# A bilinear GLU behind a dilated attention on one core: the up product copied by ScalarE in part of the steps, and due products placed earlier on VectorE

## The chip, the cores and the metric

The kernel runs on one core of a Trainium2 chip. The metric is device time in microseconds (us) of one execution. Three runs of the kernel before took 1050.43, 1051.01 and 1051.36 us, so the median is 1051.01 us. The engines are named as in the profile: PE (TensorE, with PEld for its weight loads), DVE (VectorE), ACT (ScalarE), POOL (GpSimd) and SP (the engine that issues the DMAs).

## The reference

Four layers work on x, which has 2048 tokens of 576 numbers. Layers 1 and 3 are attention (`_A_ref`), layers 2 and 4 a gated linear unit (`_B_ref`); the layers of a kind share their weights.

```
def _B_ref(x, w_gate, w_up, w_down):
    g = jnp.einsum("bsd,df->bsf", x, w_gate)
    u = jnp.einsum("bsd,df->bsf", x, w_up)
    h = g * u
    return jnp.einsum("bsf,fd->bsd", h, w_down)
...
x = x + _A_ref(_layernorm(x, axis=-1), A_wqkv, A_wo)
x = x + _B_ref(_layernorm(x, axis=-1), B_w_gate, B_w_up, B_w_down)
x = x + _A_ref(_layernorm(x, axis=-1), A_wqkv, A_wo)
x = x + _B_ref(_layernorm(x, axis=-1), B_w_gate, B_w_up, B_w_down)
```

In the attention each token looks at eight positions (its own and every second one before it) in 32 heads of 18 numbers. In the unit, F is 4608: the gate and the up product have 4608 columns each, and the down product leads back to 576.

## The kernel before, in words

**Steps.** The work is cut into 17 steps j, each one attention and one GLU on a block of tokens. Steps 0 and 1 take 128 tokens, all others 256. Steps 0 to 4 are layers 1 and 2 of the first 1024 tokens, 5 to 8 layers 3 and 4 of the same tokens, 9 to 12 and 13 to 16 the same for the last 1024 tokens.

**GLU of a step of 256 tokens** (`glu`, line 906). The 36 slices of 128 columns make 18 units of two slices; six units form a phase. A unit holds one slot: a PSUM bank for the gate (`pg`) and one for the up product (`pu`); there are four slots (the fourth pair of banks is called `acct` and `pa`). Two units at a time go through four "quarters" on PE (line 947): first quarter of unit m, of unit m+1, second quarter of m, of m+1. In each quarter two matmuls of 64 rows run beside each other, one on the gate, one on the up product. Between the first and second quarter of a unit ACT copies one number to `tok` (line 493); PE's second quarter waits for this token. After the second quarter `evac` (line 960) is called: ACT copies the gate from PSUM to `g_sb` (two buffers, line 964), and DVE multiplies the up product in PSUM with it into the bf16 tile `h` (six buffers, line 965), which also frees the slot. The down products of a phase (`down2`, line 1010, matmuls of lines 1021 and 1022) read `h` six units at a time, in two halves that hold two slots; the second half runs after the first quarter of the next phase. DVE then adds the sums to the residual stream `xf` (line 1001), which frees those two slots. Steps 0 and 1 have units of four slices, three to a phase, with matmuls of 128 rows (lines 929, 940 and 981) and no tokens.

**Attention of a step** (`attention`, line 515). PE projects (line 549), ACT brings q, k and v from PSUM to SBUF (lines 633 to 660), DVE forms the products of q and k (lines 727 to 713), takes the softmax with one exponential on ACT (lines 745 to 760), and the weights go through DRAM and back (`a_dram`, lines 791 to 796) to be spread over the partitions; in steps 0 to 2 (`on_pe`) PE spreads them instead (line 781) and ACT copies them to SBUF. Then DVE multiplies v with the weights and sums up, 16 long instructions (lines 811 and 833). PE applies the output weights (line 855), DVE adds the residual (line 846, which frees two slots), and the layer norm for the GLU follows (DVE 417, ACT 443, transposed by DMA or, in the first steps, by PE).

**What sets the order.** The program is written out by a planner (`Plan`, line 33). Every operation has an engine, a cost and dependencies; `run` takes the operation that can start first by its reckoning, and each engine runs its operations in the order in which they were taken. So the order on an engine is fixed, and an instruction that waits holds up all behind it. Each operation has a rank: an attention operation that of its step (line 1128), a GLU operation 60 (line 1130), and operations marked `due` have -1 (tokens, gate copies, products of line 965, residual additions of line 846). When the planner is about to place an operation of rank above 0, it looks for more urgent ones on the same engine (lines 119 to 125):

```
end = best[0][0] + o.cost
ahead = [(c[1].rank, c[0], c[1]) for c in urgent[o.eng] if c[1].rank < o.rank and c[1].rank < LOOK[o.eng]
         and c[0][0] < end + GUARD[o.eng] * (c[1].rank == 0) - SLACK[o.eng] * (c[1].rank < 0)
         and c[0][0] < best[0][0] + IDLE[min(max(c[1].rank, 0), 1)]]
```

LOOK is 1 on DVE, ACT and PE; SLACK is 500 (ns) on DVE and 300 on ACT; IDLE is 2000 for due operations. So a due operation is put ahead of a longer one if it can start at least 500 ns (DVE) before that one would end. Only operations whose predecessors have all been placed are candidates.

Of the kernel before, what the change touches and what calls it, by code (L numbers as in the profile page):

```python
# [10 lines left out]
ACT = mybir.ActivationFunctionType  # L11
ALU = mybir.AluOpType
# [3 lines left out]

class Op:
    __slots__ = ("eng", "cost", "fn", "deps", "order", "succ", "n", "prio", "idx", "hold", "free",
                 "lat", "margin", "ready", "end", "nbytes", "use", "pair", "need", "rank", "late", "half")


POOLQ = False
# [3 lines left out]
SLACK = {"DVE": 500, "ACT": 300, "PE": 0, "POOL": 0, "SP": 0}  # L26
IDLE = (2000, 300)
GUARD = {"DVE": 300, "ACT": 300, "PE": 600, "POOL": 0, "SP": 0}
# [4 lines left out]
class Plan:  # L33
# [11 lines left out]
        self.rd = {}  # L45

    def op(self, eng, cost, fn, r=(), w=(), prio=1, after=None, hold=None, free=None, margin=0, nbytes=0, use=None,
           pair=None, need=None, due=False, late=0, half=False):
        o = Op()
        o.rank, o.late, o.half = -1 if due else self.rank, late, half  # L50
        o.eng, o.cost, o.fn, o.prio, o.hold, o.free = eng, cost, fn, prio, hold, free
        o.margin, o.idx, o.succ, o.order, o.nbytes = margin, len(self.ops), [], set(), nbytes
        o.lat, o.use, o.pair, o.need = self.LAT[eng], use, pair, need
        d = set()
        for k in r:
            d.update(self.wr.get(k, ()))
        for k in w:
            d.update(self.wr.get(k, ()))
            d.update(self.rd.get(k, ()))
        for k in r:  # L60
            self.rd.setdefault(k, []).append(o)
        for k in w:
            self.wr[k] = [o]
            self.rd[k] = []
        d.discard(o)
        o.deps = d
        if after is not None and after not in d:
            o.order.add(after)
        for p in d | o.order:
            p.succ.append(o)  # L70
        o.n = len(d | o.order)
        self.ops.append(o)
        return o
# [10 lines left out]
    def run(self, slots):  # L84
        clock = {e: 0.0 for e in self.LAT}
        dma = {"SP": 0.0, "POOL": 0.0}
        free = {k: [(0.0, i) for i in range(v)] for k, v in slots.items()}
        cand = [o for o in self.ops if o.n == 0]
        done = 0
        half = False  # L90
        while cand:
            best = None
            urgent = {}
            for o in cand:
                t = 0.0
                for p in o.deps:
                    e = p.ready if p.eng != o.eng else p.end
                    if e > t:
                        t = e
                t += o.margin  # L100
                if o.hold is not None:
                    f = free[o.hold]
                    if not f:
                        continue
                    t = max(t, min(f)[0] + o.margin)
                if o.pair is not None:
                    if len(free["unit"]) < len(o.pair):
                        continue
                    t = max(t, min(free["unit"])[0] + o.margin)
                if o.need is not None:  # L110
                    t = max(t, o.need["at"])
                t = max(t, clock[o.eng])
                key = (t, o.prio, o.idx)
                if best is None or key < best[0]:
                    best = (key, o)
                urgent.setdefault(o.eng, []).append((key, o))
            assert best is not None, "the plan is stuck"
            o = best[1]
            if o.rank > 0:
                end = best[0][0] + o.cost  # L120
                ahead = [(c[1].rank, c[0], c[1]) for c in urgent[o.eng] if c[1].rank < o.rank and c[1].rank < LOOK[o.eng]
                         and c[0][0] < end + GUARD[o.eng] * (c[1].rank == 0) - SLACK[o.eng] * (c[1].rank < 0)
                         and c[0][0] < best[0][0] + IDLE[min(max(c[1].rank, 0), 1)]]
                if ahead:
                    best = min(ahead, key=lambda c: c[:2])[1:]
            (t, _, _), o = best
            cand.remove(o)
            if o.hold is not None:
                got = min(free[o.hold])
                free[o.hold].remove(got)  # L130
                o.use["slot"] = got[1]
            if o.pair is not None:
                for u in o.pair:
                    got = min(free["unit"])
                    free["unit"].remove(got)
                    u["at"], u["slot"] = got
            if o.eng == "PE" and self.fill and o.cost:
                if o.rank == 60:
                    self.fill = None
                else:  # L140
                    each = 430 if clock["PE"] < 5500 else 215
                    n = int((t - max(clock["PE"], 900) - 150) * 0.75 / each)
                    if n > 0:
                        self.fill(n)
            o.end = t + o.cost
            if o.eng == "PE" and o.cost:
                o.end += TURN[o.half] * (o.half != half)
                half = o.half
            clock[o.eng] = o.end
            o.ready = o.end + o.lat  # L150
            if o.nbytes:
                dma[o.eng] = max(dma[o.eng], o.end) + o.nbytes / (320.0 if o.eng == "SP" else 200.0)
                o.ready = dma[o.eng] + 2000 + o.late
            if o.free is not None:
                u = o.use
                u["last"] = max(u.get("last", 0.0), o.ready)
                u["left"] = u.get("left", 1) - 1
                if u["left"] == 0:
                    free[o.free].append((u["last"], u["slot"]))
            o.fn()  # L160
            done += 1
            for s in o.succ:
                s.n -= 1
                if s.n == 0:
                    cand.append(s)
        assert done == len(self.ops)
# [3 lines left out]
def kernel(  # L170
# [12 lines left out]
    nc = tc.nc  # L183
    _, S, D = A_x.shape
# [31 lines left out]
    def sb(name, shape, dt=BF16):  # L216
# [29 lines left out]
    oT = sb("oT", [P, KT, CH])  # L246
    n_al = nlayers // 2
    halo = [sb(f"halo{i}", [P, 2, KT, HALO]) for i in range(n_al)]
    hb = [sb(f"h{i}", [P, 2 * CH]) for i in range(NH)]
    g_sb = [sb(f"g_sb{i}", [P, 2 * CH]) for i in range(2)]  # L250
# [4 lines left out]
    pu = [psum.tile([P, 2 * CH], FP32, name=f"pu{i}") for i in range(NB)]  # L255
# [8 lines left out]
    late = {"prod": [scr[:, 2560 * i:2560 * (i + 1)].rearrange("p (a k s) -> p a k s", a=2, k=KT) for i in range(2)],  # L264
            "s1": [scr[:, o:o + 512].rearrange("p (a s) -> p a s", a=2) for o in (5120, 9216, 9728, 6656)],
            "a_c": scr[:, 6656:7168],
            "Lt": scr[:, 5632:6656].bitcast(FP32),
            "ab": scr[:, 7168:9216].rearrange("p (j s) -> p j s", j=4)}

    pl = Plan()  # L270
    op = pl.op
# [243 lines left out]
    def attention(j, la, t0, nst):  # L515
# [3 lines left out]
        on_pe = j < 3  # L519
        prio, mg = (1, 0) if fast else (3, 500 if j < 5 else 1200)  # L520
        n, sq = nst * P, nst * P // 4
# [144 lines left out]
        else:  # L666
# [12 lines left out]
           r=zk("k0", "k2", "k4", "v0", "v2", "v4"), w=hk, prio=prio)  # L679
# [18 lines left out]
        for p_ in range(W // 2):  # L698
# [26 lines left out]
            if nst == 2:  # L725
                for e in range(2):
                    op("DVE", 70 + 2.6 * n, lambda p_=p_, e=e: nc.vector.tensor_tensor(  # L727
                        late["prod"][p_ % 2][:, e, :, 0:n], qT[:, :, 0:n], kT[:, :, HALO - DIL * (2 * p_ + 1 - e):HALO - DIL * (2 * p_ + 1 - e) + n], op=ALU.mult),
                       r=qk, w=[pk], prio=prio)
            else:  # L730
                op("DVE", 70 + 5.2 * n, l1, r=qk, w=[pk], prio=prio)
            if fast:
                kw = b1.take() if p_ == 0 else dict(w=[b1.key])
                op("PE", 20 * 20, lambda p_=p_: esel(p_, lambda: [late["prod"][p_ % 2][:, :, k, :] for k in range(KT)]),
                   r=["sel", pk, "cap", "ident"], prio=0, **kw)
# [3 lines left out]
        if not fast:  # L739
            op("PE", 250 + 4 * max(45, 0.215 * n), lambda: [esel(p_, lambda p_=p_: [late["s1"][p_]]) for p_ in range(W // 2)],  # L740
               r=["sel", "s10", "s11", "s12", "s13", "cap", "ident"], prio=0, margin=mg, **b1.take())
# [5 lines left out]
        def less():  # L747
# [6 lines left out]
           r=["Lt"], w=["s13" if fast else "Lt"], prio=prio - 1)  # L754
# [19 lines left out]
        if on_pe:  # L774
            nb = 512 // (W * sq)
            for j0 in range(0, 4, nb):
# [6 lines left out]
                o = op("PE", 220, spread, r=["s13", "sel"], prio=0, margin=min(mg, 300), **b.take())  # L783
# [20 lines left out]
        for i_ in range(W):  # L804
# [8 lines left out]
            def gather(i_=i_):  # L813
                pr = late["prod"][i_ % 2][:, 0]
                nc.tensor.matmul(bo[0]()[:, 0:KF * n], lhsT=ident[:], rhs=pr[:, 0:KF, 0:n], start=(i_ == 0), stop=(i_ == W - 1))
                nc.tensor.matmul(bo[1]()[:, 0:n], lhsT=ident[:], rhs=pr[:, KF, 0:n], start=(i_ == 0), stop=(i_ == W - 1))
            op("DVE", 70 + 2.63 * n, pv, r=vk + abk, w=["oT"] if to_o else [f"prod{i_ % 2}"], prio=prio)
            if fast:
                if i_ == 0:
                    ob0 = op("PE", 0, lambda: None, w=[bo[1].key], prio=0, hold=bo[1].pool, use=bo[1].use)  # L820
# [85 lines left out]
    def glu(j, t0, nst, last):  # L906
# [53 lines left out]
        def evac(u):  # L960
            gs, hs = unit_no["n"] % 2, unit_no["n"] % NH
            unit_no["n"] += 1
            use = units[u]
            op("ACT", 490, lambda: nc.scalar.copy(g_sb[gs][:, 0:ul], pg[use["slot"]][:, 0:ul]), r=[f"wg_{j}_{u}"], w=[f"g{gs}"], prio=0, due=True)  # L964
            op("DVE", 605, lambda: nc.vector.tensor_tensor(hb[hs][:, 0:ul], pu[use["slot"]][:, 0:ul], g_sb[gs][:, 0:ul], op=ALU.mult),  # L965
               r=[f"wu_{j}_{u}", f"g{gs}"], w=[f"h{hs}"], prio=0, due=True, free="unit", use=use)
            return hs
# [204 lines left out]
```

## Time and profile before

| | |
|---|---|
| median of three runs | 1051.01 us |
| profiled execution, time / span | 1051.13 / 1049.3 us |
| PE busy | 1033.9 us (99%), 17898 matmuls |
| PEld busy | 827.8 us (79%) |
| DVE busy | 783.3 us (75%), 1446 instructions |
| ACT busy | 409.6 us (39%), 1105 instructions |
| POOL busy | 8.5 us (1%) |
| granted clock of PE | 1.00 in nearly all stretches |
| product, line 965 | 288 instructions, mean 0.686 us |
| gate copy, line 964 | 288 instructions, mean 0.586 us |
| token, line 493 | 404 instructions, mean 0.147 us |

The profiled execution took 1051.13 us, of which 1.8 us lie outside the span of the instructions. The table of groups gives for each line of the kernel the engine, the tiles, the number of instructions, their busy time and mean, and the idle time before them with what ended it. The view of waits sums up that idle time by who waited for whom. Matmuls overlap in the records, so a busy PE can hide short pauses; these show in the starts of matmuls in the timeline.

By stretches of the span, in us: from 0 to 50 PE is busy 42.1, DVE 36.6, ACT 34.4; from 84 to 380 PE is busy 292.6, DVE 259.4 and ACT 125.9 of 296; from 560 to the end PE is busy 486.2 and DVE 300.2 of 489.3.

### The profile page before, as it was taken

To read this page: it belongs to the slowest core of one execution; us is meant where nothing else is said; L and a number is where in the kernel's file an instruction comes from. 1 tells how busy PE (TensorE), PEld (TensorE's weight loads), DVE (VectorE), ACT (ScalarE), POOL (GpSimd) and SP (SyncE) were. 2 spreads that over 40 slices of the span, in tenths; PEclk is the share of its full clock that TensorE was granted. 3 is DMA by queue.
4 is the path that set the end of the run, shared out by engine and by line. 5 is a ranking of instruction groups with operands and counts; after the bars stand their busy time and mean duration, and the time that the engine had idled before them with its cause. 6 is when DMAs were issued, how large, how long until landed. Compare 5 with 4: busy or idle time off the path is not lost.

```text
span 1049.3 us, 40035 instructions
## 1 busy us (share of the span) xinstructions
PE 1033.9 (99%) x17898; PEld 827.8 (79%) x17909; DVE 783.3 (75%) x1446; ACT 409.6 (39%) x1105; POOL 8.5 (1%) x33
## 2 busy tenths in 40 slices
PE   7999999999999999999999999999999999999998
PEld 3888778789798887878887777877887788777776
DVE  7698978898899879797989573675878748833233
ACT  6643533243434553333434223434344252232231
POOL 3000000000000000000000000000000000000000
PEclk9999999999999999999999999999999999999999
DMA  8967333443425433335352625233252334343332
GB/s 253 328 209 217 88 101 110 144 108 94 99 91 134 137 76 125 107 110 164 89 130 76 179 72 132 93 103 95 88 157 82 99 91 127 117 133 98 116 103 70
DMA packets 144541, 129.67 MB, mean 124 GB/s; under 512 B 43440, under 2 KB 143728, under 8 KB 144368
## 3 DMA queue, kind: packets, MB, share of 16 engines
q1 hardware_dynamic: 144368, 127.10, 42.7%
q8 instruction: 140, 2.29, 0.9%
q14 instruction: 33, 0.27, 0.1%
HBM read 114.02 MB, written 4.19 MB: 113 GB/s over the span
## 4 chain that ended last, share of the span: by engine, by line
PE 84%; DVE 10%; DMA 3%; issue 1%; ACT 1%; SPq 1%; DVEq 0%; ACTq 0%
PE pg L953 16%; PE pu L953 16%; PE pu L1021 6%; PE acct L953 6%; PE pa L953 6%; PE pa L1021 5%; PE pg L1021 5%; PE acct L1021 4%; PE pg L549 3%; PE pu L549 3%; DVE scr L811 2%; PE pg L855 2%; DVE oT L833 2%; PE pu L929 2%; PE pg L929 1%; DMA scr<-a_dram 1%
## 5 line engine op out<-in xcount | busy, mean ns | idle before, releaser
L953 PEld LDWEIGHTS <-wg 64*128 64x128 bf16 x4320 | 393.7, 94 | 30.5 <-issue 1.7
L953 PE MATMUL pg<-xnT_B,wg 64*128 64x256 bf16 x3200 | 412.3, 269 | 1.6 <-ACT xnT_B L479 1.1
L953 PEld LDWEIGHTS <-wu 64*128 64x128 bf16 x4320 | 392.4, 94 | 25.7 <-issue 1.7
L953 PE MATMUL pu<-xnT_B,wu 64*128 64x256 bf16 x3200 | 411.4, 269 | 0.1
L1021 PEld LDWEIGHTS <-h 64*128 64x128 bf16 x2112 | 122.6, 94 | 102.5 <-DVE h L965 1.0
L1022 PE MATMUL pg<-wd,h 64*128 64x64 bf16 x1008 | 190.5, 189 | 0.0
L1022 PE MATMUL pu<-wd,h 64*128 64x64 bf16 x1008 | 190.5, 189 | 0.0
L965 DVE TENSOR_TENSOR h<-pu,g_sb 128x512 bf16<-128x512 f32 x218 | 147.1, 686 | 49.8 <-ACT g_sb L964 49.2
L493 ACT COPY tok<-pu 1x1 f32<-1x1 f32 x291 | 42.8, 147 | 322.0 <-PE pu L953 214.0
L964 ACT CAST g_sb<-pg 128x512 bf16<-128x512 f32 x218 | 126.9, 586 | 103.8 <-PE pg L953 85.0
L953 PE MATMUL acct<-xnT_B,wg 64*128 64x256 bf16 x1120 | 152.7, 269 | 0.0
L953 PE MATMUL pa<-xnT_B,wu 64*128 64x256 bf16 x1120 | 152.4, 269 | 0.2
L1021 PE MATMUL pu<-wd,h 64*128 64x512 bf16 x576 | 149.5, 377 | 0.4 <-ACT tok L493 0.3
L1021 PE MATMUL pg<-wd,h 64*128 64x512 bf16 x576 | 149.3, 377 | 0.2 <-DVE h L965 0.2
L1021 PE MATMUL pa<-wd,h 64*128 64x512 bf16 x480 | 123.8, 377 | 0.0
L1021 PE MATMUL acct<-wd,h 64*128 64x512 bf16 x480 | 123.7, 377 | 0.0
L1022 PEld LDWEIGHTS <-h 64*128 64x128 bf16 x2112 | 121.6, 95 | 1.2 <-issue 0.4
L549 PEld LDWEIGHTS <-wqkv 64*128 64x128 bf16 (+1 forms) x2030 | 102.8, 94 | 15.8 <-issue 3.5
L727 DVE TENSOR_TENSOR scr<-qT,kv 128x1280 bf16<-128x1280 bf16 x112 | 88.5, 816 | 25.7 <-ACT kv L633 25.7
L953 PE MATMUL pg<-xnT_B,wgu_t 64*128 64x256 bf16 x400 | 107.6, 269 | 0.0
L953 PE MATMUL pu<-xnT_B,wgu_t 64*128 64x256 bf16 x400 | 107.6, 269 | 0.0
L549 PE MATMUL pg<-xnT_A,wqkv 64*128 64x256 bf16 (+2 forms) x863 | 100.0, 265 | 1.1 <-DVE xf L1001 0.8
(172 smaller groups left out, 1497.3 us busy)
## 6 DMA issues: line engine op xcount, KB each, us to landing
wd<-in_B_w_down_dram SPq DMA_DIRECT2D x306, 288.0 KB, 4.5
scr<-a_dram SPq DMA_DIRECT2D x56, 128.0 KB, 2.7
wg<-in_B_w_gate_dram SPq DMA_DIRECT2D x6, 768.0 KB, 9.5
wu<-in_B_w_up_dram SPq DMA_DIRECT2D x6, 768.0 KB, 11.2
xb<-in_A_x_dram SPq DMA_DIRECT2D x7, 288.0 KB, 2.9
out_dram<-xf SPq DMA_DIRECT2D x14, 144.0 KB, 3.3
a_dram<-scr SPq DMA_DIRECT2D x14, 128.0 KB, 2.0
scr<-in_A_wqkv_dram SPq DMA_DIRECT2D x4, 288.0 KB, 5.2
```

Of the source, the lines that this page charges most:

```text
L493: box["at"] = nc.scalar.copy(tok[0:1, :], src())
L549: return nc.tensor.matmul(bank(p_, u)[0:m, e * n:(e + 1) * n], lhsT=wqkv[r_, k, w0:w0 + m], rhs=xnT_A[r_, k, c0:c0 + n], start=start, stop ...
L727: op("DVE", 70 + 2.6 * n, lambda p_=p_, e=e: nc.vector.tensor_tensor(late["prod"][p_ % 2][:, e, :, 0:n], qT[:, :, 0:n], kT[:, :, HALO - DI ...
L811: nc.vector.tensor_tensor(js(dst), js(vT[:, :, o0:o0 + n]), abw, op=ALU.mult)
L833: op("DVE", 70 + 2.63 * n, lambda i_=i_: nc.vector.tensor_tensor(oT[:, :, 0:n], oT[:, :, 0:n], late["prod"][i_ % 2][:, 0, :, 0:n], op=ALU. ...
L855: return nc.tensor.matmul(bank(hh, us[i])[:, 0:HD], lhsT=oT[rows, t, i * P:(i + 1) * P], rhs=wo_p[rows, t, hh * HD:(hh + 1) * HD], start=( ...
L929: nc.tensor.matmul(pt[:, e * n:(e + 1) * n], lhsT=w_[:, k, ft * P:(ft + 1) * P], rhs=xT[:, k, 0:n], start=(first and k == 0 and e == 0), s ...
L953: return nc.tensor.matmul(ps[:, e * n:(e + 1) * n], lhsT=w_, rhs=xT[rows, k, 0:n], start=(first and e == 0 and k == 0), stop=(not first an ...
L964: op("ACT", 490, lambda: nc.scalar.copy(g_sb[gs][:, 0:ul], pg[use["slot"]][:, 0:ul]), r=[f"wg_{j}_{u}"], w=[f"g{gs}"], prio=0, due=True)
L965: op("DVE", 605, lambda: nc.vector.tensor_tensor(hb[hs][:, 0:ul], pu[use["slot"]][:, 0:ul], g_sb[gs][:, 0:ul], op=ALU.mult), r=[f"wu_{j}_{ ...
L1021: return [lambda: nc.tensor.matmul((pg, pu)[i][use["slot"]][:], lhsT=lhs, rhs=wt[rows, e % 2, 0:512], start=first, stop=fin, skip_group_ch ...
L1022: lambda: nc.tensor.matmul((pg, pu)[i][tl["slot"]][:, 0:TL], lhsT=lhs, rhs=wt[rows, e % 2, 512:D], start=first, stop=fin, skip_group_check ...
```

## The change

In steps 1 and 2 for all units, and in steps 3, 4 and 5 for the units with `u % 6 < 4` (of each phase of six, all but the last two), `evac` has one more instruction: ACT copies the up product from PSUM into `h` as bf16 right after the gate copy, which frees the slot, and DVE multiplies `h` by `g_sb` in place, all in SBUF. The planner is told 490 for the copy and 350 for the product. That is 9 units in step 1, 18 in step 2 and 12 in each of steps 3 to 5, 63 of the 288. The other units are as before.

The planner's rule is changed in two ways. For DVE operations of rank 3 and above (the attention of steps 3 and later) the 500 ns of SLACK are no longer taken off: a due operation goes ahead if it can start before the other would end. And an operation can have a `risk`, by which both bounds of the rule reach further; it is 2000 for the first product of v and weights (line 811, i_ of 0) in the steps whose weights come by DMA (3 to 16).

```diff
     def op(self, eng, cost, fn, r=(), w=(), prio=1, after=None, hold=None, free=None, margin=0, nbytes=0, use=None,
-           pair=None, need=None, due=False, late=0, half=False):
+           pair=None, need=None, due=False, late=0, half=False, risk=0):
...
             if o.rank > 0:
-                end = best[0][0] + o.cost
+                end = best[0][0] + o.cost + o.risk
                 ahead = [(c[1].rank, c[0], c[1]) for c in urgent[o.eng] if c[1].rank < o.rank and c[1].rank < LOOK[o.eng]
-                         and c[0][0] < end + GUARD[o.eng] * (c[1].rank == 0) - SLACK[o.eng] * (c[1].rank < 0)
-                         and c[0][0] < best[0][0] + IDLE[min(max(c[1].rank, 0), 1)]]
+                         and c[0][0] < end + GUARD[o.eng] * (c[1].rank == 0) - SLACK[o.eng] * (c[1].rank < 0 and (o.rank < 3 or o.eng != "DVE"))
+                         and c[0][0] < best[0][0] + o.risk + IDLE[min(max(c[1].rank, 0), 1)]]
...
-            op("DVE", 70 + 2.63 * n, pv, r=vk + abk, w=["oT"] if to_o else [f"prod{i_ % 2}"], prio=prio)
+            op("DVE", 70 + 2.63 * n, pv, r=vk + abk, w=["oT"] if to_o else [f"prod{i_ % 2}"], prio=prio, risk=2000 * (i_ == 0 and not on_pe))
...
             op("ACT", 490, lambda: nc.scalar.copy(g_sb[gs][:, 0:ul], pg[use["slot"]][:, 0:ul]), r=[f"wg_{j}_{u}"], w=[f"g{gs}"], prio=0, due=True)
+            if j in (1, 2) or 0 < j < 6 and u % 6 < 4:
+                op("ACT", 490, lambda: nc.scalar.copy(hb[hs][:, 0:ul], pu[use["slot"]][:, 0:ul]), r=[f"wu_{j}_{u}"], w=[f"h{hs}"], prio=0, due=True,
+                   free="unit", use=use)
+                op("DVE", 350, lambda: nc.vector.tensor_tensor(hb[hs][:, 0:ul], hb[hs][:, 0:ul], g_sb[gs][:, 0:ul], op=ALU.mult),
+                   r=[f"g{gs}", f"h{hs}"], w=[f"h{hs}"], prio=0, due=True)
+                return hs
             op("DVE", 605, lambda: nc.vector.tensor_tensor(hb[hs][:, 0:ul], pu[use["slot"]][:, 0:ul], g_sb[gs][:, 0:ul], op=ALU.mult),
                r=[f"wu_{j}_{u}", f"g{gs}"], w=[f"h{hs}"], prio=0, due=True, free="unit", use=use)
             return hs
```

More of the change, by code (lines that the diff above doesn't have):

```diff
@@ L18 @@
     __slots__ = ("eng", "cost", "fn", "deps", "order", "succ", "n", "prio", "idx", "hold", "free",
-                 "lat", "margin", "ready", "end", "nbytes", "use", "pair", "need", "rank", "late", "half")
+                 "lat", "margin", "ready", "end", "nbytes", "use", "pair", "need", "rank", "late", "half", "risk")
 POOLQ = False
@@ L47, in op @@
     def op(self, eng, cost, fn, r=(), w=(), prio=1, after=None, hold=None, free=None, margin=0, nbytes=0, use=None,
[L48 removed]
+           pair=None, need=None, due=False, late=0, half=False, risk=0):
         o = Op()
[L50 removed]
+        o.rank, o.late, o.half, o.risk = -1 if due else self.rank, late, half, risk
         o.eng, o.cost, o.fn, o.prio, o.hold, o.free = eng, cost, fn, prio, hold, free
```

## The prediction

> **What bounds the kernel now.** I read the busy times first, then PE's own waits, then the timelines around the longest of them. The page's first part has PE at 99%:
>
> ```profile
> PE 1033.9 (99%) x17898; PEld 827.8 (79%) x17909; DVE 783.3 (75%) x1446; ACT 409.6 (39%) x1105; POOL 8.5 (1%) x33
> ```
>
> PE's work is not touched by the change, so only its pauses can be won. The view of waits, for PE alone, shows how few there are (total us, number, longest us):
>
> ```profile
> PE pg L953 <- ACT xnT_B L479: 1.1, 1, 1.1
> ...
> PE pg L549 <- DVE xf L1001: 0.8, 1, 0.8
> ...
> PE pg L953 <- DVE xf L846: 0.5, 1, 0.5
> ...
> PE pu L549 <- DVE xf L1001: 0.5, 1, 0.5
> ...
> PE pu L1021 <- ACT tok L493: 0.3, 1, 0.3
> PE pg L1021 <- DVE h L965: 0.2, 1, 0.2
> ```
>
> Since matmuls overlap in the records, I counted pauses a second way, from the starts in PE's timeline. Pairs of 256 columns start 0.109 us apart (0.4265 ns a column); where a start comes over 60 ns later than the columns before it explain, the excess is a pause. They add up to 29.2 us. Of these 14.5 lie in the first 50 us, before any instruction of the change. Between 50 and 111 us there are 4, nearly all pauses of 0.09 to 0.22 us between kinds of matmul, which stay. What is left to win is a short list: 1.31 us at 120.6 (line 953 waits for xnT_B), 0.98 + 0.62 at 143.6 (line 549 waits for two slots), 0.26 at 273.0, 0.30 at 281.8, 0.16 at 301.6, 0.64 + 0.26 at 312.4, 0.16 at 369.5, 0.41 at 404.1, 0.34 at 464.6, 0.34 at 512.5 (0.08 + 0.26), all behind DVE, and 0.26 at 406.6 and 0.43 at 557.1 behind a token on ACT. The sum is 6.5 us, 0.6% of the time. DVE's timeline shows the kind that the new rule aims at:
>
> ```profile
> 311.15 0.82 DVE L727 TENSOR_TENSOR scr<-qT,kv 128x1280 bf16<-128x1280 bf16 x1
> 311.88 0.45 DVE L846 TENSOR_TENSOR xf<-pg,xf 128x288 f32<-128x288 f32 x1
> 312.25 0.45 DVE L846 TENSOR_TENSOR xf<-pu,xf 128x288 f32<-128x288 f32 x1
> ```
>
> PE's line 953 starts at 312.38, as the second residual addition lets a slot go; an attention product of 0.82 us stood in front.
>
> **A faster DVE starts no GLU sooner after step 3.** The last residual of attention 3 starts at 157.6 and the first gate copy of GLU 3 at 188.8: a lead of 31 us; for step 4 it is 38 (210.6 and 248.8), for step 5 56 (263.2 and 318.9). So time saved on DVE there is worth only the local waits, and time lost on DVE costs nothing until 31 us are used up.
>
> **The copies, step by step.** Taken away: a product that reads PSUM. Added: one of the same shape, all bf16 in SBUF, and an ACT copy like the gate's. The rows:
>
> ```profile
> L965 DVE TENSOR_TENSOR h<-pu,g_sb 128x512 bf16<-128x512 f32 x218 | 147.1, 686 | 49.8 <-ACT g_sb L964 49.2
> L964 ACT CAST g_sb<-pg 128x512 bf16<-128x512 f32 x218 | 126.9, 586 | 103.8 <-PE pg L953 85.0 <-PE pu L940 11.3 <-PE pg L929 3.7
> L712 DVE TENSOR_TENSOR scr<-scr 128x512 bf16<-128x512 bf16 (+1 forms) x64 | 26.4, 412 | 1.6
> ```
>
> From start to start the product takes 0.60 (403.40 to 404.00); an addition of 512 bf16 numbers in SBUF 0.35 before an independent successor (310.80 to 311.15). So 0.25 us a unit are saved, 63 x 0.25 = 16 us of DVE. ACT gets 63 x 0.49 (two copies back to back take 1.05) = 31 us; between 84 and 380 us it is busy 125.9 of 296, and would be at 53%. It does not become the bound on average, but its queue is in order, and what stands behind a copy matters: tokens, attention copies and the exponential. `h` itself comes 0.2 us later (0.49 + 0.59 + 0.42 against 0.59 + 0.69); in step 2, where a phase's last two units are copied too, the half of the down products begins with the first eight slices, 8 x 0.245 = 1.96 us before the fifth unit's `h` is read, which hides it.
>
> The Trainium skill speaks against such a copy: by "VectorE: DVE Perf Modes", section "Rules for kernel authors", an elementwise operation on a matmul's output either takes the slow rate of PSUM or is copied to SBUF first if many operations follow. Here one follows, and by the rows the copy costs 0.49 to save 0.25. By this rule alone the change would lose 0.24 us a unit, 15 us of engine time; the traces put the saving on the busier engine.
>
> *Step 1, the 1.31 us at 120.6.* GLU 2 starts when attention 2 is through DVE. Its output products wait for the sums that end at 106.2. Five products lie between 94.5 and 105.4, so 5 x 0.25 = 1.25 us would go. But just before, ACT is full:
>
> ```profile
> 84.03 1.05 ACT L964 CAST g_sb<-pg 128x512 bf16<-128x512 f32 x2
> 84.98 0.60 ACT L633 CAST scr<-pa 128x512 bf16<-128x512 f32 x1
> ...
> 88.95 0.43 ACT L445 ACTIVATE xn<-xf,nmr,rstd 128x64 bf16<-128x64 bf16 x1
> 89.28 0.57 ACT L633 CAST scr<-pa 128x512 bf16<-128x512 f32 x1
> ```
>
> DVE then waits 2.1 us for that last copy. Three up copies fall into this stretch; at 0.49 they can hold it up by 1.5 us. Bounds: 1.25 gained, 1.5 lost (0.25 net after the saving). I take 0.3 gained.
>
> *The 1.60 us at 143.6.* DVE stood 3.9 us before the first product with the weights, waiting for their DMA, and the additions that free the slots (line 1001) were placed behind six long instructions. They are not due, so the new rule does not lift them. Earlier work of attention 3 would help, but its exponential now stands behind two up copies. Bounds: all 1.6 gained, 0.5 lost; I take 0.4 gained. For 273.0, 281.8 and 301.6, waits behind a DVE in these same steps, 0.3 of 0.7 goes.
>
> **Due operations first.** The rows 312.4, 369.5, 404.1, 464.6 and 512.5 (together 2.15 us) are due operations behind one of 0.7 to 0.8 us. At 404.1 the product ran 1.7 us after its gate copy ended (401.69 to 403.40), since the plan and the chip drift apart, and 0.5 us more of foresight does not mend all of that. I take 1.3 gained; bounds 0.3 and 2.15. What is next behind each is PE itself. The price is a DVE that stands idle up to 0.5 us before such a product. With 14 steps this is some us of DVE, hidden by the lead. For the first product with the weights, `risk` lets every due product that is already in the plan go first; behind it wait the 15 long instructions of that attention and its output products, also under the lead. No DMA's issue is added or moved by hand; SP's order follows the plan. Cost of new misplacements: 0.3, from 0 to 1.5 (the longest wait of this list).
>
> **Tokens.** A token that is late stops PE at once. In pairs of quarters ACT now has two tokens (0.15), two gate and two up copies (0.49) in 3.9 us: 2.3 us, which fits. Where attention work of 1.25 us (lines 443 and 445) stands between, a token can come late. The two waits in the trace cost 0.26 and 0.43. There are 27 pairs with copies in steps 2 to 5; two late ones at 0.25 give 0.5. Bounds: 0 and 27 x 0.35 = 9.5.
>
> **Sum**, on the profiled execution's own 1051.13 us: -0.3 - 0.4 - 0.3 - 1.3 + 0.3 + 0.5 = -1.5, which gives 1049.6 us. That execution lies 0.1 above the median of the runs shown, so I leave it at that; the 1.8 us outside the span stay.
>
> **Rivals.**
> *Nearly the whole list goes*: DVE's 16 us come at the right places, 120.6 and 143.6 close (2.9), the due list too (2.15): 1051.1 - 5.1 = 1046.0. For it: DVE is busy 259 of 296 us in these steps. Against: the ACT rows above.
> *ACT takes the place of DVE, slower than before*: place, the tokens of steps 2 to 5. It decides once ACT is over a quarter (0.87 to 1.09 us) behind, that is when one attention instruction and two copies pile up. With half the pairs late, 14 x 0.35 = 4.9, less the 1.3 of the due list and nothing else: 1054.7. This is also where the copy rule named above would show.
> *The edits do nothing that lasts*: a late operation moves to another place and the gains are eaten: 1051.1.
>
> **How the numbers follow.** Forecast 0.46 (1048.2 to 1050.6), nearly the whole list 0.20, nothing that lasts 0.14, slower 0.20. The range leaves out half of the slower cases and a little of the best: 1045.8 to 1053.8. About 0.2%, 2.1 us, is what a measurement here tells from no change. Faster than 1048.9: the second case and a third of the forecast, 0.36. Slower than 1053.1: 0.21 with what the forecast's tail adds. Between: 0.43.
>
> **What would show it.** Right: products of 0.41 in SBUF in 63 places, DVE some 10 to 16 us less busy between 84 and 380 us; the waits of lines 953 and 1021 on lines 846 and 965 gone; DVE idle before products up. Wrong: PE waits on `tok` that add up to over 2 us, or a wait for xnT_B that has grown; or a new wait of PE on line 1001, behind products that were put first.

## The result and the profile after

The changed kernel takes 1043.97 us (median of six runs, 1043.88 to 1044.20), the kernel before 1050.86 us beside it. The ratio is 0.9935, with a 95% interval from 0.9922 to 0.9948: 6.9 us faster. The forecast said 1049.6 us with a range down to 1045.8, so the direction of the forecast held and its size did not: the measured time lies below the whole range.

The busy times of the page after:

```profile
span 1042.2 us, 40091 instructions
...
PE 1031.5 (99%) x17899; PEld 807.7 (77%) x17909; DVE 775.6 (74%) x1446; ACT 438.5 (42%) x1168; POOL 8.9 (1%) x33
```

There are 63 more ACT instructions, as many DVE instructions as before, and a span that is 7.1 us shorter. PE's own waits after (total us, number, longest us):

```profile
PE acct L1144 <- DVE g_sb L1148: 1.2, 1, 1.2
PE pu L467 <- ACT xn L443: 1.1, 1, 1.1
PE pu L719 <- DVE scr L704: 1.1, 2, 0.7
PE pu L815 <- DVE scr L811: 0.6, 1, 0.6
...
PE pu L549 <- ACT tok L493: 0.3, 1, 0.3
```

Of the six lines that the prediction shows from this view, none is left. The first four lines here lie in the first 50 us, which the change does not reach; the last is the one token wait that remains.

The groups of the product and the copies after (in after.py, line 964 is the gate copy, 966 the up copy, 968 the product in SBUF, 971 the product from PSUM):

```profile
L971 DVE TENSOR_TENSOR h<-pu,g_sb 128x512 bf16<-128x512 f32 x170 | 116.5, 690 | 59.5 <-ACT g_sb L964 58.9
L966 ACT CAST h<-pu 128x512 bf16<-128x512 f32 x47 | 28.3, 602 | 0.0
L968 DVE TENSOR_TENSOR h<-h,g_sb 128x512 bf16<-128x512 bf16 x63 | 26.4, 422 | 23.1 <-ACT h L966 22.3
```

The product in SBUF takes 0.42 us, as the addition of the same shape did before, and the up copy 0.60. The last column shows the price on DVE: it stood idle 23.1 us before these products, 22.3 of them waiting for the up copy.

To compare kernels I counted the pauses of PE in each trace as the prediction did (start to start, above what the columns explain) and kept those over 0.13 us after the first 100 us, so that the short ones between kinds of matmul fall out. "Lag" is the mean time from the end of a gate copy to the start of its product; where the up product is copied, the up copy lies inside it. Median and ratio are of all runs, span and pauses of the one execution that was profiled.

| kernel | ratio to before, 95% interval | median us | span us | pauses us | lag us |
|---|---|---|---|---|---|
| before | | 1050.86 | 1049.3 | 7.13 | 0.365 |
| after | 0.9935 [0.9922, 0.9948] | 1043.97 | 1042.2 | 0.84 | 0.219 |
| risk_only | 1.0004 [0.9990, 1.0019] | 1050.63 | 1050.4 | 7.21 | |
| copies_only | 0.9977 [0.9967, 0.9988] | 1047.30 | 1047.3 | 4.99 | 0.445 |
| rule_only | 0.9953 [0.9940, 0.9965] | 1045.46 | 1043.7 | 1.94 | |
| slack_only | 0.9948 [0.9935, 0.9960] | 1044.70 | 1042.9 | 1.38 | 0.127 |
| after_again | 0.9935 [0.9924, 0.9947] | 1043.86 | 1042.1 | 0.95 | 0.225 |
| copies_slack | 0.9936 [0.9924, 0.9947] | 1044.02 | 1042.2 | 0.46 | |
| prod_first | 0.9956 [0.9944, 0.9969] | 1045.88 | 1044.0 | 2.57 | 0.127 |
| res_first | 0.9980 [0.9970, 0.9989] | 1048.68 | 1047.1 | 4.53 | 0.328 |
| slack_250 | 0.9968 [0.9957, 0.9980] | 1046.10 | 1044.9 | 3.21 | 0.188 |
| copies12_slack | 0.9961 [0.9948, 0.9975] | 1045.56 | 1043.7 | 2.09 | |
| copy_everything | 0.9955 [0.9943, 0.9968] | 1044.88 | 1043.0 | 1.01 | |
| both_act | 0.9978 [0.9969, 0.9987] | 1047.67 | 1045.6 | 3.94 | |
| slack_only_again | 0.9938 [0.9922, 0.9954] | 1045.06 | 1043.2 | 1.47 | 0.129 |
| idle_copies_slack | 0.9994 [0.9985, 1.0003] | 1051.21 | 1049.8 | 7.35 | |
| copies345_slack | 0.9934 [0.9918, 0.9950] | 1044.40 | 1043.4 | 1.92 | |
| both_all_ranks | 0.9952 [0.9936, 0.9969] | 1046.46 | 1045.0 | 2.48 | |

The experiments ran in four groups of four, in the order of the table, each group on one chip beside the kernel before. Spans go with pauses: from before to after the pauses fall by 6.3 us and the span by 7.1, and the span less the pauses lies between 1041.1 and 1043.2 us in all eighteen rows. The profiled executions of `copies_only` and `risk_only` took 2.1 and 1.5 us more than the median of their kernels. The kernel before had medians of 1050.4, 1050.8, 1049.6 and 1051.8 us in these groups, so ratios are to be compared inside a group first.

### The profile page after: what moved, and what is told of

The parts are those of the page before. It is cut to its first block, busy times and chain, and to the rows that moved or that the text cites. A ratio compares the mean times of both kernels' runs of the same rounds, so it can differ in the third digit from the quotient of the medians.

```text
span 1042.2 us, 40091 instructions
## 1 busy us (share of the span) xinstructions
PE 1031.5 (99%) x17899; PEld 807.7 (77%) x17909; DVE 775.6 (74%) x1446; ACT 438.5 (42%) x1168; POOL 8.9 (1%) x33
## 4 chain that ended last, share of the span: by engine, by line
PE 96%; DVE 1%; ACT 1%; DMA 1%; issue 0%; SPq 0%; DVEq 0%; ACTq 0%
PE pu L953 19%; PE pg L953 18%; PE pu L1027 11%; PE pg L1027 7%; PE pa L953 7%; PE acct L953 7%; PE pg L549 4%; PE pu L549 4%; PE pa L1027 2%; PE pg L855 2%; PE pu L929 2%; PE pg L929 1%; PE pg L987 1%; PE acct L1027 1%; PE pg L1028 1%; PE pu L1028 1%
## 5 line engine op out<-in xcount | busy, mean ns | idle before, releaser
L953 PEld LDWEIGHTS <-wu 64*128 64x128 bf16 x4320 | 387.8, 94 | 27.6
L1027 PE MATMUL pu<-wd,h 64*128 64x512 bf16 x888 | 228.0, 377 | 0.0
L1027 PE MATMUL pg<-wd,h 64*128 64x512 bf16 x888 | 227.8, 377 | 0.0
L1027 PEld LDWEIGHTS <-h 64*128 64x128 bf16 x2112 | 117.4, 94 | 107.6
L971 DVE TENSOR_TENSOR h<-pu,g_sb 128x512 bf16<-128x512 f32 x170 | 116.5, 690 | 59.5 <-ACT g_sb L964 58.9
L1028 PE MATMUL pg<-wd,h 64*128 64x64 bf16 x744 | 140.6, 189 | 0.0
L1028 PE MATMUL pu<-wd,h 64*128 64x64 bf16 x744 | 140.6, 189 | 0.0
L1028 PEld LDWEIGHTS <-h 64*128 64x128 bf16 x2112 | 115.1, 95 | 0.6
L549 PE MATMUL pg<-xnT_A,wqkv 64*128 64x256 bf16 (+2 forms) x908 | 106.0, 266 | 0.5 <-ACT wqkv L358 0.3
L549 PE MATMUL pu<-xnT_A,wqkv 64*128 64x256 bf16 (+1 forms) x888 | 104.5, 266 | 1.1 <-DVE wqkv L358 0.4
L833 DVE TENSOR_TENSOR oT<-oT,scr 128x1280 bf16<-128x1280 bf16 (+1 forms) x112 | 89.8, 802 | 2.8
```

The lines of the kernel that those rows point to most:

```text
L549: return nc.tensor.matmul(bank(p_, u)[0:m, e * n:(e + 1) * n], lhsT=wqkv[r_, k, w0:w0 + m], rhs=xnT_A[r_, k, c0:c0 + n], start=start, stop ...
L833: op("DVE", 70 + 2.63 * n, lambda i_=i_: nc.vector.tensor_tensor(oT[:, :, 0:n], oT[:, :, 0:n], late["prod"][i_ % 2][:, 0, :, 0:n], op=ALU. ...
L953: return nc.tensor.matmul(ps[:, e * n:(e + 1) * n], lhsT=w_, rhs=xT[rows, k, 0:n], start=(first and e == 0 and k == 0), stop=(not first an ...
L1027: return [lambda: nc.tensor.matmul((pg, pu)[i][use["slot"]][:], lhsT=lhs, rhs=wt[rows, e % 2, 0:512], start=first, stop=fin, skip_group_ch ...
L1028: lambda: nc.tensor.matmul((pg, pu)[i][tl["slot"]][:, 0:TL], lhsT=lhs, rhs=wt[rows, e % 2, 512:D], start=first, stop=fin, skip_group_check ...
```

## The experiments

**First group: the parts of the change alone.** `copies_only` undoes both edits of the rule:

```diff
-                         and c[0][0] < end + GUARD[o.eng] * (c[1].rank == 0) - SLACK[o.eng] * (c[1].rank < 0 and (o.rank < 3 or o.eng != "DVE"))
+                         and c[0][0] < end + GUARD[o.eng] * (c[1].rank == 0) - SLACK[o.eng] * (c[1].rank < 0)
...
-            op("DVE", 70 + 2.63 * n, pv, r=vk + abk, w=["oT"] if to_o else [f"prod{i_ % 2}"], prio=prio, risk=2000 * (i_ == 0 and not on_pe))
+            op("DVE", 70 + 2.63 * n, pv, r=vk + abk, w=["oT"] if to_o else [f"prod{i_ % 2}"], prio=prio)
```

> The 63 up copies of the change alone, the planner's rule as before (500 ns taken off everywhere, no risk). Theory 1, each part closes its own pauses: the copies close those at 120.6 and 143.6 us (2.9) and those at 273.0, 281.8 and 301.6 us (0.7), so 1050.9 - 3.6 = 1047.3 us, and the pauses behind line 846 and 965 at 312, 369, 404, 464 and 512 us stay. Theory 2, the rule does it all and the copies only move work: 1050.9 us or above. Theory 3, the copies do nearly all: 1045 us or below.

Measured: 0.9977, 2.4 us on the 1050.35 us of its chip. The median, 1047.30 us, is the very number of theory 1, but that was reckoned from 1050.9 us. The copies do something alone, and theories 2 and 3 fall. In the trace the pauses that theory 1 names, 120.6, 143.6 and the three behind, are gone, but others came in their place, such as 1.16 us at 325.0, and the 0.34 us at 464.6 grew to 0.86 at 461, both behind DVE. The lag grew to 0.445 us because the up copy lies inside it: it is 0.866 for the 63 copied units and 0.327 for the others.

`rule_only` keeps the rule and turns the copies off (`if False:` in place of the condition on j and u).

> No up copies; the planner's rule as after the change (500 ns no longer taken off for DVE operations of rank 3 and above, risk 2000 at the first product with the weights). Theory 1, each part closes its own pauses: 2.2 us behind lines 846 and 965 and up to 0.7 behind tokens go, the two large early ones stay: 1048.0 to 1048.7 us. Theory 2, the rule does it all: 1044.5 us or below. Theory 3, the copies do nearly all: 1050 us or above.

Measured: 0.9953, 4.9 us. That is about twice what theory 1 gave the rule and short of theory 2. Without any copy the pause at 143.6 is gone and the one at 120.6 is down to 0.36 us at 117.0, so the pauses did not belong to the parts as I had it.

`slack_only` has the rule without risk and without copies:

> No up copies and no risk; only the 500 ns are no longer taken off for DVE operations of rank 3 and above. Theory 1: as with the whole rule, 1048.0 to 1048.7 us, since the risk was priced at nothing. If it is the risk that counts within the rule: 1050 us or above here, and the kernel with the risk alone below that.

Measured: 0.9948, 5.5 us. `risk_only` is its complement:

> No up copies, 500 ns taken off as before; only the risk of 2000 at the first product with the weights in steps 3 to 16. Theory 1: 1050.9 us, no change, since no pause of the list was put down to this DMA but the 1.6 us at 143.6, and there the additions of line 1001 are not due and not lifted. If DVE's standing before that product is what holds PE up: 1049 us or below.

Measured: 1.0004, no change. The pauses add up to as much as before (7.21 us), though the one at 143.6 is gone and others stand elsewhere, such as 1.2 us near 351. So the risk wins nothing, and the dropped 500 ns carry most of the gain: 5.5 of 6.9 us here, and 6.5 us when the same kernel ran again on the chip of the fourth group.

How the rule works can be seen where attention 2 ends. DVE in `slack_only`:

```profile
106.74 1.55 DVE L727 TENSOR_TENSOR scr<-xf 128x1280 bf16<-128x1280 bf16 x2
108.32 0.69 DVE L708 TENSOR_TENSOR scr<-scr 128x1024 bf16<-128x1024 bf16 x1
108.97 0.46 DVE L846 TENSOR_TENSOR xf<-pg,xb 128x288 f32<-128x288 f32 x1
```

and before:

```profile
108.30 0.69 DVE L708 TENSOR_TENSOR scr<-scr 128x1024 bf16<-128x1024 bf16 x1
109.02 0.42 DVE L712 TENSOR_TENSOR scr<-scr 128x512 bf16<-128x512 bf16 x1
109.48 0.43 DVE L713 TENSOR_TENSOR scr<-scr 128x512 bf16<-128x512 bf16 x1
109.83 0.45 DVE L846 TENSOR_TENSOR xf<-pg,xb 128x288 f32<-128x288 f32 x1
```

The residual additions of attention 2 go ahead of two sums of attention 3 (rank 3) and come 0.86 us earlier. They lead to GLU 2, whose start was the 1.31 us pause. The halves of the rule, below, bear this out: with residual additions alone put first the pause is down to 0.36 us, with products alone it stays at 1.31.

At 143.6 something else happened. The additions of line 1001 (1007 in the new numbering) that PE waited for come no earlier in `slack_only`: 143.97 against 142.91 us. But PE no longer asks for their slots there. Before, it started the projections of attention 4 (line 549) at 143.6; in `slack_only` it does the first of them from 134.7 to 138.7 and the next from 146.3. So the order of PE's work is another one. Why the planner arrives at it no run shows. It is not that products are placed earlier, for both halves of the rule, products alone and residual additions alone, give this order.

No other trace of the record has a pause there before line 549, not even that of `risk_only`, where PE and DVE have the order of before in this stretch. DVE's first product with the weights there, before and in `risk_only`:

```profile
138.24 0.83 DVE L811 TENSOR_TENSOR oT<-xf,scr 128x1280 bf16<-128x1280 bf16 x1 [3.87 <-DMA scr<-a_dram]
```

```profile
136.97 0.82 DVE L811 TENSOR_TENSOR oT<-xf,scr 128x1280 bf16<-128x1280 bf16 x1 [2.16 <-DMA scr<-a_dram]
```

The weights' write to DRAM (`a_dram`) took 3.63 us to land in the one trace and 1.71 in the other, the additions came at 142.91 and 141.64, and PE did not wait in the second. So these 1.60 us hung on how long one DMA took in the execution that was profiled. A list of pauses from one execution can have such entries, and what they are worth in the median of many runs is open.

**Second group: the whole change again, the copies with the rule, and the rule's two halves.**

> The whole change, on the chip of the next three, so that they can be set beside it. 0.9935 of before. If the copies add to the rule, 1 to 1.5 us below copies_slack without risk is not to be expected (the two should be equal, the risk alone gave nothing), and both should lie 1 us or more below a kernel with the rule alone (0.9948 to 0.9953). If the copies add nothing to the rule, all lie within 0.5 us of the rule alone.

> The copies and the dropped 500 ns, without the risk. Theory that the risk is idle: equal to the whole change within 0.5 us. Theory that the risk matters once products come one ACT copy later and a late DMA would hold more: 1 us or more above it.

Measured: 0.9935 and 0.9936. The risk is idle beside the copies too. For the halves, due operations are told apart by their planned cost (370 for a residual addition):

```diff
-  - SLACK[o.eng] * (c[1].rank < 0 and (o.rank < 3 or o.eng != "DVE"))
+  - SLACK[o.eng] * (c[1].rank < 0 and (o.rank < 3 or o.eng != "DVE" or c[1].cost == 370))
```

> No copies, no risk; the 500 ns dropped for products of line 965 alone, kept for the residual additions of line 846 (told apart by their cost in the plan). Theory by the list of pauses: behind line 965 lie 0.41 and 0.16 us only, so 1050.4 us. Theory that the products of 288 units matter throughout, since each late one shifts PE's order and the plan drifts from the chip: most of the 5.5 us, 1046 us or below.

> The other half: the 500 ns dropped for the residual additions of line 846 alone, kept for products. Theory by the list: behind line 846 lie 0.90, 0.16, 0.34 and 0.34 us, and at 120.6 us the additions came 0.86 us earlier when the rule was dropped for both, so up to 1.3 more: 1047.9 to 1049.2 us. Theory that products matter throughout: 1049.5 us or above.

(`res_first` has `!= 370`.) Measured: products alone 0.9956, 4.6 us on 1050.8; residual additions alone 0.9980, 2.1 us. The residual additions are worth what the expectation made of the list of pauses, though not place by place: new waits behind products stand in their trace, 1.1 us in three. The products are worth eight times the 0.57 us that stood behind line 965 in the list. With them first, the lag falls from 0.365 to 0.127 us and the products that start over 1 us after their gate copy from 31 to 5; in `res_first` they are still 21. Against before, the pauses of `prod_first` are 4.6 us fewer: the 1.60 at 143.6, 0.57 behind products, 0.69 behind tokens, 0.7 behind residual additions, 0.3 behind an attention instruction (line 749, at 281.8) and short ones. So most of its gain lies in pauses that did not end with a product. What is left is 1.31 at the start of GLU 2, 1.01 behind residual additions and 0.26 behind line 1007.

**Third group: the dose, and ACT.**

> No copies, no risk; for DVE operations of rank 3 and above 250 ns are taken off in place of 500 or 0. Theory that what counts is how far ahead a due operation is seen (about 0.74 us long ones in front of it): between the two, 1047 to 1049 us. Theory that any other order of the plan happens to suit better: no order in the dose, as likely below 1045 or above 1050.5 us.

Measured: 0.9968, between the two (1 at 500 ns, 0.9948 and 0.9938 at 0). The lag goes 0.365, 0.188, 0.127 us, the pauses 7.13, 3.21, 1.4. So the gain follows the dose, which speaks against an order that only happens to suit; with three doses, on different chips, it does not rule it out.

> The dropped 500 ns with the up copies of steps 1 and 2 alone (27 units), no risk. If the copies' share on top of the rule (0.7 to 1 us) lies at the early pauses near 117 and 127 us, which are still there with the rule alone (0.36 and 0.52), this equals the whole change: 1043.9 us. If it lies in steps 3 to 5 (0.34 at 391 us and small ones), it stays at 1044.8 us or above.

Measured: 0.9961, 1045.56 us. The copies of steps 1 and 2 alone show no gain on top of the rule: the pauses near 117 and 127 us go, but 0.68 us behind line 1007 at 377.1 and 0.46 at a token at 248.8 stand there instead.

`copy_everything` copies all 288 units (`if True:`).

> The rule and the risk as in the change, but all 288 units copied by ACT, step 0 too. Theory of the forecast's slower rival: ACT falls behind, tokens come late in a part of the 135 pairs and 1.5 us or more is lost against the whole change, 1045.5 us or above, with PE waiting on tok. Theory that ACT has room everywhere once due operations go first: 1044.5 us or below.

Measured: 0.9955, 1044.88 us, between the two expectations. PE waits on no token over 0.13 us; one wait of 0.85 us for a product at 368.7 is left. It did not run on one chip with the whole change, so a loss of up to some 2 us by the ratios is open; one of several us on tokens is ruled out.

`both_act` drops ACT's 300 ns too (the condition is `o.rank < 3` alone).

> Copies and the dropped 500 ns, no risk, and ACT's 300 ns dropped too for rank 3 and above. If the token waits that are left (0.46 at 357 us) come from long attention copies placed in front of tokens: 1043.5 us. If they come from a quarter that follows its token too closely: no change, 1043.9 us. If ACT's idling delays the attention that its exponential feeds: above 1045 us.

Measured: 0.9978, 1047.67 us; by the ratios 4 us worse than with ACT's 300 ns kept (0.9936). Of the pauses 1.36 us are behind attention copies of line 633: in the two larger ones ACT had stood 0.58 and 0.33 us waiting for PE with a token, in front of a copy that PE needs. Another 1.84 us are at tokens, four of 0.46. These are not late through ACT, which stood idle 0.45 to 1.00 us before each, waiting for PE: the second part of a projection follows the first at once in PE's order, and the token between them has no time. The token wait that is left in the whole change is of the same kind (ACT, in after.py):

```profile
355.97 0.15 ACT L493 COPY tok<-pu 1x1 f32<-1x1 f32 x1
356.02 0.62 ACT L753 ACTIVATE scr<-scr 128x512 f32<-128x512 f32 x1
357.06 0.15 ACT L493 COPY tok<-pu 1x1 f32<-1x1 f32 x1 [0.41 <-PE pu L549]
```

Going first is not good in itself; on ACT the attention copies free PE's slots as well.

**Fourth group: what the copies add.**

> The dropped 500 ns alone, the same kernel as slack_only, as the mark for the others on this chip: 0.9948 of before, 1044.7 to 1045 us.

Measured: 0.9938, 1045.06 us. In `idle_copies_slack` ACT copies the 63 up products into `h`, and the product reads PSUM again, writes over them and frees the slot. The copy is work for nothing.

```diff
+                use["left"] = 2
...
-                op("DVE", 350, lambda: nc.vector.tensor_tensor(hb[hs][:, 0:ul], hb[hs][:, 0:ul], g_sb[gs][:, 0:ul], op=ALU.mult),
-                   r=[f"g{gs}", f"h{hs}"], w=[f"h{hs}"], prio=0, due=True)
+                op("DVE", 605, lambda: nc.vector.tensor_tensor(hb[hs][:, 0:ul], pu[use["slot"]][:, 0:ul], g_sb[gs][:, 0:ul], op=ALU.mult),
+                   r=[f"wu_{j}_{u}", f"g{gs}"], w=[f"h{hs}"], prio=0, due=True, free="unit", use=use)
```

> The dropped 500 ns and ScalarE's 63 up copies, but their result is not used: the product still reads PSUM behind the copy, overwrites it and frees the slot. So ScalarE's load and the later product stand alone, without the shorter product and the earlier slot. Theory that the copies' gain is VectorE's time or the earlier slot: slower than the rule alone, by 0.3 us or more. Theory that it is another order of the plan, whose sign is chance: as likely below the rule alone as above it. If ScalarE's load had been dear: 3 us or more above.

Measured: 0.9994, 1051.21 us: 6.2 us above the rule alone. So ACT's copies, with the product and the slot that now wait for them, cost about as much as the rule wins, and the shorter product with the earlier slot pays that back. Whether it pays more is not shown: the whole change (0.9935) never ran beside the rule alone (0.9948 and 0.9938), the medians on different chips lie 0.7 to 1.2 us apart, and the intervals overlap. PE's waits in this kernel:

```profile
PE pg L953 <- DMA xnT_B<-xn: 2.5, 1, 2.5
...
PE pu L953 <- DVE xf L1008: 0.9, 2, 0.5
PE pu L1029 <- DVE h L969: 0.6, 1, 0.6
PE pa L467 <- ACT xn L443: 0.6, 1, 0.6
```

The largest is the start of GLU 4, which waits for its normed input. Its attention's last residual addition starts at 233.05 us (210.6 before). The norm's factors are ready by 236.9, but ACT, with gate and up copies in front and two waits for PE among them, applies them only at 242.73:

```profile
241.37 0.58 ACT L964 CAST g_sb<-pg 128x512 bf16<-128x512 f32 x1 [0.68 <-PE pg L953]
242.25 0.58 ACT L964 CAST g_sb<-pg 128x512 bf16<-128x512 f32 x1 [0.29 <-PE pg L953]
242.73 0.87 ACT L443 ACTIVATE xn<-xf,nmr,rstd 128x576 bf16<-128x576 f32 x1
```

Here the lead of attention over the GLU was used up, 38 us before. Which of the two, the shorter product or the earlier slot, pays more was not separated.

> The dropped 500 ns and the 36 copies of steps 3 to 5. If the copies' share on top of the rule lies in these steps: 0.7 us or more below the rule alone. If it needs all 63 or is chance of the plan: within 0.5 us of the rule alone, or above.

Measured: 0.9934, 1044.40 us, 0.7 us below the rule alone by the medians, inside the intervals. Its list of pauses (1.92 us) is no shorter than that of the rule alone (1.47) in the profiled executions, so where this lies stays open.

> Copies, no risk, and the 500 ns dropped on VectorE for every rank. The attention of steps 1 and 2 has no lead over PE, so theory: VectorE's standing before products comes through there and costs 0.5 to 2 us against the whole change (1044.5 to 1046 us). If due first is right everywhere: 1043.5 us or below.

Measured: 0.9952, 1046.46 us. By the ratios that is 1.8 us above the whole change, as the first theory had it; the time is 0.5 above the range it gave. One pause shows it: GLU 2 starts 1.76 us late.

```profile
PE pg L953 <- ACT xnT_B L479: 1.6, 1, 1.6
```

The attention of steps 1 and 2 has no lead, for GLU 2 starts as soon as its normed input is there; the last residual addition of attention 2 comes at 111.44 us, 109.11 in the whole change. This speaks for the limit at rank 3 in the rule. None of the versions beats the whole change beyond its interval.

## Why the prediction was right and wrong

*What can be won.* Right: PE's work was untouched, and the gain is the pauses. After 100 us the pauses over 0.13 us went from 7.13 to 0.84, and the listed 6.5 us were nearly all there was. Set against the terms of the sum, place by place (in us, gains positive):

| place | forecast | pauses before | after |
|---|---|---|---|
| start of GLU 2, 120.6 | 0.3 | 1.31 | 0 |
| 143.6 | 0.4 | 1.60 | 0 |
| 273.0, 281.8, 301.6 | 0.3 | 0.72 | 0 |
| the due list, 312.4 to 512.5 | 1.3 | 2.15 | 0 |
| tokens | -0.5 | 0.69 | 0.46 |
| new misplacements | -0.3 | none | 0 |

The places were right, and each term that had bounds came out at the best one or past it. The range, though, had its low end at 1045.8, where the rival that took "nearly the whole list" had only 5.1 of the 6.5 us; the whole list would have been 1044.6, and the result is 0.6 below that.

*Due operations first.* This is the step that failed, and by its size: "I take 1.3 gained; bounds 0.3 and 2.15". The rule alone gave 5.5 us. The direction was right, and so was the mechanism where it was followed (a due operation behind one of 0.7 to 0.8 us). What was wrong was to give the rule only the pauses that end with a due operation: the two large ones, 2.9 us, went to the copies, and the additions at 143.6 were left there because "the new rule does not lift them". It does not, but without any copy the pause at 143.6 went wholly and the one at 120.6 down to 0.36. The residual half, 2.1 us, lay inside the bounds, in part by luck: with it alone these two places went the same way, which the term did not hold, and new waits took part of that back. The product half stood in the term with one pause, the 0.41 us at 404.1 (another of 0.16 at 301.6 went to the copies), and gave 4.6. The working held PE's order fixed, while the new order of DVE came with a new order of PE. A pause ended by line 1001, 846 or 479 may also come from products that were late before, since these additions and the attention wait in the same DVE queue; the trace of `prod_first` fits that, but no run separates it from the new order of PE, so how the 4.6 us divide stays open. A warning was in the text: the product that ran 1.7 us after its gate copy. One such row was a sign for 31 over 1 us; the lag of all 288 was not taken. A smaller misreading: PE's start at 312.38 follows the end of the first residual addition (311.88 + 0.45), not the second.

*Step 1, the 1.31 us at 120.6.* The forecast was 0.3 gained, because ACT would hold up the spreading. The delay shows in the trace after: the first product with the weights came at 91.30 in place of 89.89, 1.4 us later (the text had 1.5). Yet the sums ended at 104.98 in place of 106.2, so the stretch between became 2.6 us shorter. The shorter products account for some 0.75 of that, for only three of the five still lie in it; two were placed behind the last sum (about 1.2), and the additions of line 992 (998 after) ran in front, while DVE waited (0.7). The working had kept DVE's order. The pause went wholly. The rule did most of it alone, to 0.36 us, with 0.5 us new near 127; with the copies alone it closed as well.

*The 1.60 us at 143.6.* Forecast 0.4; it went. Under the rule alone that is by the new order of PE, with the additions no earlier; under the copies alone PE's order is the old one and the additions come at 140.01 (142.91 before), in the whole change at 139.41. As `risk_only` shows, a shorter DMA was enough to end this pause, so part of this gain may be chance of the profiled execution.

*The copies.* Prices right: 0.42 and 0.60 us against 0.41 and 0.59; ACT is busy 151.9 of 296 us between 84 and 380, 51% (53% forecast). The three groups of products are busy 180.8 us, 195.1 before: 14.3 less for 16. The sign "10 to 16 us less busy between 84 and 380 us" failed: DVE is 26.7 us less busy there (232.8 for 259.4), with 27 instructions fewer, since work moved out of the stretch; over the whole span it is 7.7 less. The rule of the Trainium skill that the prediction weighed, in "VectorE: DVE Perf Modes", section "Rules for kernel authors" (accept the slow rate of PSUM, or copy a matmul's output to SBUF first if many operations follow), would have had the change lose. The price that it reckons with is there: 6.2 us in `idle_copies_slack`, where the copy's result is not used. But with the product in SBUF and the earlier slot, one operation behind the copy was enough to pay for it (`copies_slack` at 0.9936, the rule alone at 0.9938 and 0.9948).

*Tokens.* Forecast 0.5 lost on top of the 0.69 that stood there; the trace after has 0.46 at one token, 0.23 less than before. So this term was wrong, in sign too. The one wait has about the size that was forecast, but not its mechanism: no copy or attention work stood in front of that token, ACT was idle. With all 288 units copied no token wait is over 0.13 us. The slower rival would have had its place elsewhere: in `idle_copies_slack` ACT's load costs at the start of a GLU and behind DVE, hardly at tokens (0.14 us).

*The risk and the price of going first.* The risk at nothing: right. New misplacements, 0.3 forecast: none shows; the two pauses of 0.22 and 0.16 that are left beside the token have their like before. DVE stands idle 116.5 us before products, 80.8 before: 36 us more, and it is hidden: of PE's pauses that are left only the token's is new. The lead at GLU 3 is 31 us again (155.5 and 186.2), at GLU 6 it went from 76 to 40 us (335.4 and 375.0). The statement that nothing is lost until the lead is used up holds in steps 3 and later, and the two kernels in which a lead was missing (`both_all_ranks`) or used up (`idle_copies_slack`) show what follows.

## What to carry to other kernels

Where a planner fixes each engine's order, do not price a rule of order by the pauses that end with the operations that it moves alone: a pause shows the last wait of a chain, a new order moves the chain, and a pause can hang on one DMA of the execution that was profiled. Look also at how late these operations are in all places, from the trace (end of the producer to start of the consumer, all of them). That is a sign and not a price: `copy_everything` has a mean lag of 0.634 us, with the copy in it, and is faster than the kernel before. An engine with a lead can be made to stand idle for the sake of short operations that the bounding engine needs, as long as the lead lasts; without a lead the same rule costs. A copy that only shifts work to a freer engine has to be paid for by what it makes shorter or sets free, since its load on an in-order queue, with the product and the slot that waited for it, cost 6 us here.

## What had not been expected

The whole change varies less from execution to execution than the kernel before. On the chip of the second group, 17 runs of the kernel before went from 1047.92 to 1053.44 us, 5 of the whole change from 1043.78 to 1044.21; on the chip of the first group `risk_only` went from 1048.31 to 1055.60 and `slack_only` from 1044.46 to 1045.40. The granted clock was 0.99 or more in all of these. Fewer pauses do not always go with less spread: `both_act`, with 3.94 us of pauses, went from 1047.23 to 1048.21 in 11 runs, and `copies12_slack`, with 2.09, from 1044.46 to 1046.80 in 5. What it is that varies was not tested; one thing that does is the time a write to `a_dram` takes to land, 1.7 to 3.7 us among the 14 of the trace before.
